# A gated linear recurrence and a SwiGLU block on one core: weights narrowed with one VectorE pass fewer, group 0 begun chunk by chunk, and one more pair of chunks through the 15-product scheme

## The chip, the cores and the metric

The kernel runs on one core of one Trainium2 chip. A core has TensorE (PE, matmuls; the loading of its stationary operand is shown apart as PEld), VectorE (DVE), ScalarE (ACT), GpSimd (POOL) and SyncE (SP), which here only issues DMAs. The metric is the device time of one execution in microseconds (us). The median of three runs of the kernel before is 701.25 us (699.18 to 704.5).

## The reference

```python
def _attn_ref(q, k, v, a_re, a_im):            # (B, H, S, D) = (4, 8, 768, 48)
    mag = np.sqrt(a_re * a_re + a_im * a_im)
    scale = np.minimum(mag, 0.999) / (mag + 1e-06)
    a_re_n, a_im_n = (a_re * scale, a_im * scale)
    for t in range(S):                          # S_re, S_im start at zero
        ar, ai = (a_re_n[:, :, t, :, None], a_im_n[:, :, t, :, None])
        new_re = ar * S_re - ai * S_im
        new_im = ar * S_im + ai * S_re
        kv = np.einsum('bhd,bhe->bhde', k[:, :, t], v[:, :, t])
        S_re, S_im = (new_re + kv, new_im)
        y[:, :, t] = np.einsum('bhd,bhde->bhe', q[:, :, t], S_re)
    return y

def _moe_ref(x, w_gate, w_val, w_out, rms_g):   # x = y as (3072, 384); d_ff = 1536
    rms = np.sqrt(np.mean(x * x, axis=-1, keepdims=True) + 1e-06)
    xn = x / rms * rms_g
    g = xn @ w_gate
    silu = g * (1.0 / (1.0 + np.exp(-g)))
    return silu * (xn @ w_val) @ w_out
```

The activations are float32. The three weight matrices come as float64 and reach the chip as pairs of 32-bit words.

## The kernel before

**Tiling.** The 4 x 768 time steps are cut into 24 chunks of 128 (`C`). Units (`UNITS`) prepare the gates: chunks 0 and 1 are units of one chunk, the others of two. Two chunks form a group (`GROUPS`, 12 of them), which goes through the SwiGLU block together.

**Stages of a chunk.** `gates(u)` turns a_re and a_im into magnitudes and phases (ACT, with several activation tables, and DVE scans), multiplies q and k with them (`rot`), and SP's DMAs reorder the result into the tile `kq`, which the heads read (six DMAs a chunk). `attend(n)` computes masked scores from `kq` (PE, then a COPY_PREDICATED into `am` on DVE), the output y (bank 6, which order and trace number as 71), and the state carried to the next chunk (PE transposes, copies `kt` on ACT, `state` on DVE). The stage "norm" squares y (`sq`), sums it by a matmul with `ones`, makes the mean square `ssv` on DVE and its power -1/2 `rs` on POOL, spreads that over the partitions, by a matmul with `ident` for the first four chunks, and writes the transposed, normalised chunk into `xT`.

**The SwiGLU block.** `feed(g)` is the plain form: for each of six pairs of 128 hidden columns it multiplies `xT` with `wg` and `wv` (12 matmuls with 256 moving columns), ACT takes the silu into `sg`, DVE multiplies into `hT`, and at the end `hT` meets `wo` (24 matmuls of 384 columns for groups 0 and 1). `joint(g)` is the form for the later groups: the 18 block products of a pair of row blocks with the weights' blocks are replaced by 15 products (`PRODUCTS`, in the order of `STEPS`), whose left factors are sums of blocks of `xT` (`X_SUMS`, 12 additions of 128 columns on DVE for each group) and whose right factors are sums of blocks of `wg` and `wv` (`W_SUMS`). `forms()` makes the latter once, 14 sums for each of the two matrices, 512 columns each, partly in place: it can only follow the last plain `feed`. The output product is in seven parts instead of eight (`down`) from group 2 (`FIRST`) on. `PLAIN = 3`: groups 0 to 2 take `feed`, groups 3 to 11 `joint`.

**Weights.** POOL's DMAs fetch them in 12 pieces (six of `wg` and `wv`, 1536 columns of double words each, and six of `wo`, 768 columns) into places in `wo` and `hT` that are free at the start; a piece is issued when the piece before the previous has landed. `narrow(i)` makes float32 of a piece: ACT scales the low words (`Copy`, scale 2^-29), DVE shifts the high words left by 3 (TENSOR_SCALAR), joins the sign and clears two bits (SCALAR_TENSOR_TENSOR), and adds the low word (an integer addition; order shows it as ISA, the trace as CUSTOM_DVE_ANT_0). For groups 0 and 1 the gain `rms_g` (`gcol`) is applied to y; the stage "scale" after group 1 multiplies it into `wg` and `wv`, before the sums. Near the end, `look` reads all weights once more to see that they lie in the range for which this is exact.

**What sets the order.** `Flow` holds every operation with its engine, an assumed duration and a due time, and writes each engine's instructions in the order of a list schedule made while the program is built; on the chip each engine runs its own list in that order and waits by semaphores. Two tables change that order without changing the work: the DMA rate that `dma` assumes, and `flow.shift`, which moves due times by stage and chunk. `send_decays(u)` of units 0 and 1 makes a product `own[u]` on DVE (shown as `ot<-ends,ot`) that a small matmul on PE reads. While PE waits at the start, `flow.warm` puts matmuls on `rot0` without use into its list.

Of the kernel before, what the change touches and what calls it, by code (L numbers as in the profile page):

```python
# [12 lines left out]
BF16 = mybir.dt.bfloat16  # L13
AF = mybir.ActivationFunctionType
# [4 lines left out]
P = 128  # L19
# [698 lines left out]
def fast(tc, ctx, qT, kT, v, a_re, a_im, w_gate, w_val, w_out, rms_g, out, H, bad):  # L718
# [19 lines left out]
    PLAIN = 3  # L738
    WIDE = 12
    SOLO = 6  # L740
# [96 lines left out]
    def dma(o, x, eng="SP", slow=0.0, **kw):  # L837
# [4 lines left out]
        load = n / row * (0.006 + 50.3e-6 * row) / 16  # L842
# [4 lines left out]
        op["packet"] = max(0.07, 0.006 + 50.3e-6 * row * (2 if eng == "POOL" and row == 2048 else 1))  # L847
# [26 lines left out]
    gcol = room("gcol", [P, ND])  # L874
    zeros = room("zeros", [P, 2 * C])
# [71 lines left out]
    dma(gcol, rms_g.rearrange("(c p) -> p c", p=P))  # L947

# [45 lines left out]
    HALVED = ()  # L994

    def narrow(i):
# [8 lines left out]
        act(lo, lo.bitcast(U32), AF.Copy, scale=2.0 ** -29)  # L1005
        step = n // 2 if i in HALVED else n
        for f in range(0, n, step):
            to_, lo_, hi_ = (x[:, :, f:f + step] for x in (t, lo, hi))
            add("DVE", [(nc.vector.tensor_scalar, (),
                         dict(out=to_, in0=hi_, scalar1=3, scalar2=None, op0=ALU.logical_shift_left))],  # L1010
                0.15 + 0.52e-3 * rows * step, [hi_], [to_])
            stt(to_, hi_, 0x3FFFFFFF, to_, ALU.bitwise_or, ALU.bitwise_and)
            tt(to_, to_, lo_, ALU.add)
# [69 lines left out]
    def send_decays(u):  # L1083
        ns = UNITS[u]
        if u < 2:
# [117 lines left out]
    def attend(n):  # L1203
# [75 lines left out]
        if unit_of[n] in LIGHT:  # L1279
            for j in range(ND):  # L1280
                act(yg[:, j], yT[:, j], AF.Copy, scale=gcol[:, j:j + 1])
# [38 lines left out]
    FIRST = 2  # L1320
    WARM = 62.0
# [14 lines left out]
    def feed(g, xT):  # L1336
# [26 lines left out]
        for i in range(2):  # L1363
# [5 lines left out]
            act(ots[i], o, AF.Copy)  # L1369
# [181 lines left out]
    for n in range(N):  # L1551
# [10 lines left out]
        if n == GROUPS[g][-1] and g < WIDE:  # L1562
# [4 lines left out]
            if g == FIRST - 1:  # L1567
# [21 lines left out]
    for in_, limit, op in ((ef, P_MIN, ALU.is_ge), (ef, 1.0, ALU.is_le), (range_, 0.0, ALU.is_le),  # L1589
# [18 lines left out]
        ("attend", 8): 0.6, ("attend", 9): 3.8, ("attend", 11): 3.3, ("attend", 14): 1.6, ("attend", 15): -6.6,  # L1608
        ("attend", 22): 1.5, ("attend", 23): 0.2, ("feed", 4): 13.5, ("feed", 5): 2.3, ("form", 4): 15.0,
        ("form", 12): -0.4, ("look", 3): 1.7, ("look", 6): 70.9, ("look", 7): 45.5, ("look", 8): 38.3,  # L1610
        ("look", 9): 46.0, ("look", 10): 2.2, ("look", 11): -0.3, ("look", 12): 4.4, ("look", 13): 74.9,
        ("look", 14): 75.0, ("look", 15): 69.7, ("look", 16): 45.1, ("look", 17): -3.0, ("norm", 7): 7.5,
        ("norm", 19): -0.1, ("norm", 20): -0.4, ("norm", 21): -1.4, ("norm", 22): -1.4, ("root", 0): -2.0,
        ("root", 3): 21.5, ("root", 8): -10.8, ("rot", 2): -4.7, ("rot", 9): -1.1, ("scale", 0): 2.7,
        ("size", 3): 2.2, ("size", 4): -9.6, ("size", 6): -8.3, ("size", 9): 14.4, ("size", 11): -1.5,
        ("state", 2): -0.3, ("state", 4): -17.0, ("state", 6): -16.7, ("state", 8): -4.3, ("state", 13): -37.5,
        ("state", 14): -11.8, ("state", 15): -8.0, ("state", 19): -14.7, ("state", 22): -0.3, ("turn", 9): 5.8,
# [57 lines left out]
```

## Time and profile before

| | value |
|---|---|
| median of the runs shown | 701.25 us (699.18, 701.25, 704.5) |
| profiled execution, own time | 701.28 us |
| its span, first to last instruction | 699.5 us (1.78 us lie around it) |
| PE busy | 657.1 us, 94% of the span |
| DVE, ACT, POOL busy | 559.4, 477.9 and 59.7 us (80%, 68%, 9%) |
| mean granted TensorE clock | 0.989 |
| chain that ended last, by engine | PE 79%, DVE 7%, ACT 6%, DMA 3%, SP's queue 2%, issue 2% |

All operations are recorded by one line of `Flow` (L715), so rows are told apart by tiles and shapes, not by lines. A matmul of float32 shows as two instructions. Times in the timeline are microseconds from the first instruction; the mean of a group is the time from an instruction's start to its end, and neighbours overlap a little.

### The profile page before, as it was taken

The numbers are of one execution on the slowest core, as the hardware profiler recorded it, in microseconds if no ns is written. First come the engines' busy times: TensorE is split into PE (matmuls) and PEld (weight loads), VectorE is DVE, ScalarE is ACT, GpSimd is POOL, SyncE is SP. The second block draws the span as 40 slices with busy tenths as digits, with TensorE's granted clock in tenths as the row PEclk, the third lists the DMA queues.
The fourth block names the chain that finished last, engine by engine and source line by source line (L and its number), as shares of the span: only waits on it lengthen the run. The fifth ranks groups of instructions, "written<-read, shape, count | busy, mean of one in ns | idle before, by whom it ended". The sixth has DMA issues, their size and how long they took to land.

```text
span 699.5 us, 18714 instructions
## 1 busy us (share of the span) xinstructions
PE 657.1 (94%) x7792; PEld 607.5 (87%) x7792; DVE 559.4 (80%) x1017; ACT 477.9 (68%) x807; POOL 59.7 (9%) x108
## 2 busy tenths in 40 slices
PE   0698999999999999999999999999999998999995
PEld 0587867886889999998999999999999998999995
DVE  8989888869888788888788889888898896356462
ACT  8657777898654675574675684675674884688884
POOL 3122100011000001000101010001000010000000
PEclk9989999999999999999999999999999999999999
DMA  9995462535424243434504334424623543834422
GB/s 292 291 290 178 154 166 75 148 65 106 111 57 103 60 82 62 134 77 86 128 17 80 96 70 96 126 60 86 133 53 75 119 97 112 250 94 145 149 72 91
DMA packets 104012, 81.98 MB, mean 117 GB/s; under 512 B 41936, under 2 KB 94416, under 8 KB 103920
## 3 DMA queue, kind: packets, MB, share of 16 engines
q1 hardware_dynamic: 98560, 64.78, 34.6%
q0 software_dynamic: 4416, 15.35, 10.3%
q8 instruction: 62, 1.02, 0.6%
q10 hardware_dynamic: 944, 0.59, 0.3%
q14 instruction: 30, 0.25, 0.1%
HBM read 55.84 MB, written 4.72 MB: 87 GB/s over the span
## 4 chain that ended last, share of the span: by engine, by line
PE 79%; DVE 7%; ACT 6%; DMA 3%; SPq 2%; issue 2%; POOL 0%; DVEq 0%; ACTq 0%
PE bank L715 79%; SPq L715 2%; DMA kq<-kin 2%; ACT turns L715 2%; ACT L715 1%; DVE hT L715 1%; DVE rot L715 1%; ACT t L715 1%; DVE wv L715 1%; DVE turns L715 1%; DMA in<-in_a_im_dram 1%; DVE wg L715 1%; DMA in<-in_a_re_dram 1%; DVE t L715 1%; DVE in L715 0%
## 5 line engine op out<-in xcount | busy, mean ns | idle before, releaser
L715 PE MATMUL bank<-wo,hT 128*128 128x192 f32 (+1 forms) x696 | 143.7, 352 | 0.9 <-DVE hT L715 0.9
L715 PEld LDWEIGHTS bank<-wo,hT 128*128 128x128 f32 x696 | 115.5, 191 | 13.3 <-DVE hT L715 1.8
L715 PE MATMUL bank<-xT,wg 128*128 128x128 f32 (+1 forms) x504 | 98.2, 330 | 0.0
L715 PE MATMUL bank<-xT,wv 128*128 128x128 f32 (+1 forms) x504 | 94.3, 321 | 0.0
L715 PEld LDWEIGHTS bank<-xT,wg 128*128 128x128 f32 x504 | 80.2, 194 | 7.4 <-issue 0.4
L715 PEld LDWEIGHTS bank<-xT,wv 128*128 128x128 f32 x504 | 79.1, 192 | 5.9 <-ACT turns L715 0.2
L715 ACT ACT_TABLE_LOAD x51 | 65.4, 1283 | 7.3 <-DVE t L715 2.8
L715 ACT ACTIVATE hT<-bank 128x512 f32<-128x512 f32 x90 | 52.4, 594 | 25.9 <-PE bank L715 23.1
L715 POOL TENSOR_TENSOR rs<-ssv,mhalf 128x1 f32<-128x1 f32 x24 | 20.6, 858 | 479.0 <-DVE ssv L715 428.3
L715 ACT ACTIVATE sg<-bank 128x512 f32<-128x512 f32 (+1 forms) x72 | 38.9, 540 | 21.1 <-PE bank L715 17.9
L715 DVE TENSOR_TENSOR hT<-hT 128x768 f32<-128x768 f32 (+1 forms) x58 | 50.5, 871 | 1.1
L715 ACT ACTIVATE bank<-bank 128x512 f32<-128x512 f32 x54 | 31.5, 583 | 26.8 <-PE bank L715 18.9
L715 ACT ACTIVATE kt<-bank 128x384 f32<-128x384 f32 x40 | 19.5, 489 | 43.9 <-PE bank L715 34.8
L715 DVE COPY_PREDICATED am<-causal,bank 128x512 f32<-128x512 int32 x48 | 34.7, 731 | 16.0 <-PE bank L715 15.9
L715 PE MATMUL bank<-yg,wg 128*128 128x128 f32 x288 | 45.7, 281 | 0.0
L715 PE MATMUL bank<-sums,hT 128*128 128x192 f32 x240 | 44.7, 328 | 0.1
L715 PE MATMUL bank<-yg,wv 128*128 128x128 f32 x288 | 43.9, 275 | 0.0
L715 DVE TENSOR_TENSOR hT<-bank,hT 128x512 f32<-128x512 f32 x45 | 30.9, 688 | 14.8 <-ACT bank L715 7.8
L715 PEld LDWEIGHTS bank<-kq 96*32 96x32 f32 x1536 | 31.3, 112 | 12.6 <-issue 4.5
L715 PE MATMUL bank<-kq 96*32 96x128 f32 (+3 forms) x1536 | 37.0, 240 | 5.4 <-DMA kq<-kin 3.6
L715 ACT ACTIVATE turns<-in 128x768 f32<-128x768 f32 (+1 forms) x39 | 30.4, 791 | 13.8 <-DVE kin L715 12.7
L715 PEld LDWEIGHTS bank<-sums,hT 128*128 128x128 f32 x240 | 39.3, 190 | 0.5 <-DVE yg L715 0.2
(216 smaller groups left out, 1417.4 us busy)
## 6 DMA issues: line engine op xcount, KB each, us to landing
kq<-rot SPq DMA_DIRECT2D x90, 128.0 KB, 2.5
kq<-kin SPq DMA_DIRECT2D x54, 128.0 KB, 2.7
kin<-in_q_dram SPq DMA_DIRECT2D x24, 192.0 KB, 3.2
kin<-in_k_dram SPq DMA_DIRECT2D x24, 192.0 KB, 3.4
out_dram<-ot SPq DMA_DIRECT2D x23, 192.0 KB, 2.8
in<-in_a_re_dram SPq DMA_DIRECT2D x11, 384.0 KB, 4.3
in<-in_a_im_dram SPq DMA_DIRECT2D x11, 384.0 KB, 4.2
vn<-in_v_dram SPq DMA_DIRECT2D x20, 192.0 KB, 2.6
```

The source lines that it names most:

```text
L715: fn(*args, **kw)
```

## The change

- `narrow`: the SCALAR_TENSOR_TENSOR is gone. ACT writes the scaled low word as 16 bits and, in a second operation (`Sign`), the sign as a bfloat16 (1 or -1) into the other half of the same word; DVE shifts and adds. This makes the weights half as large; the factor is put back by `gate_col` and `val_col` (from `gcol`) and by the scale of the copies into `ots`.
- `PLAIN = 2`, and with it `LATER = 4`; `SOLO = 4`: group 2 takes `joint`, `forms()` follows group 1, and chunks 4 and 5 use the single buffers of the later chunks.
- `feed` of group 0: the first two of its six blocks (`SPLIT`) multiply each chunk by itself (24 matmuls of 128 columns in place of 12 of 256).
- The DMA rate assumed by the schedule is 41e-6 us a byte and engine instead of 50.3e-6, and `flow.shift` is another table.

```diff
-    PLAIN = 3
+    PLAIN = 2
-    SOLO = 6
+    SOLO = 4
...
-        load = n / row * (0.006 + 50.3e-6 * row) / 16
+        load = n / row * (0.006 + 41e-6 * row) / 16
...
+    MORE = [1.0 if x.dtype == FP32 else 2.0 for x in (w_gate, w_val, w_out)]
+    act(gate_col, gcol, AF.Copy, scale=MORE[0])
+    act(val_col, gcol, AF.Copy, scale=MORE[1] * MORE[2])
...
-        act(lo, lo.bitcast(U32), AF.Copy, scale=2.0 ** -29)
-        step = n // 2 if i in HALVED else n
-        for f in range(0, n, step):
-            to_, lo_, hi_ = (x[:, :, f:f + step] for x in (t, lo, hi))
-            add("DVE", [(nc.vector.tensor_scalar, (),
-                         dict(out=to_, in0=hi_, scalar1=3, scalar2=None, op0=ALU.logical_shift_left))],
-                0.15 + 0.52e-3 * rows * step, [hi_], [to_])
-            stt(to_, hi_, 0x3FFFFFFF, to_, ALU.bitwise_or, ALU.bitwise_and)
-            tt(to_, to_, lo_, ALU.add)
+        low, high = (places[i].bitcast(d).rearrange("p (c f four) -> p c f four", f=n, four=4)[:, :, :, k]
+                     for d, k in ((U16, 0), (BF16, 1)))
+        act(low, lo.bitcast(U32), AF.Copy, scale=2.0 ** -29)
+        act(high, hi.bitcast(FP32), AF.Sign)
+        add("DVE", [(nc.vector.tensor_scalar, (),
+                     dict(out=t, in0=hi, scalar1=3, scalar2=None, op0=ALU.logical_shift_left))],
+            0.15 + 0.52e-3 * rows * n, [hi], [t])
+        tt(t, t, lo, ALU.add)
...
+    SPLIT = 2
...
+                if g == 0 and b < SPLIT:
+                    for t in range(2):
+                        list_ = []
+                        for i in range(2):
+                            f = b * 2 + i
+                            for d in range(ND):
+                                list_.append((o[:, i * T + t * C:i * T + (t + 1) * C],
+                                              w_[:, f // 4, d, f % 4 * P:(f % 4 + 1) * P],
+                                              xT[:, d, t * C:(t + 1) * C], d == 0, d == ND - 1))
+                        dur = 2 * ND * mm_time(C)
+                        clock[0] += dur * SPREAD
+                        mms(list_, dur, due=clock[0] - (1 - t) * dur)
+                    continue
...
-            act(ots[i], o, AF.Copy)
+            act(ots[i], o, AF.Copy, scale=MORE[2])
...
-                    for w_ in (wg, wv):
+                    for w_, col in ((wg, gate_col), (wv, val_col)):
                         for d in range(ND):
-                            act(w_[:, f, d], w_[:, f, d], AF.Copy, scale=gcol[:, d:d + 1])
+                            act(w_[:, f, d], w_[:, f, d], AF.Copy, scale=col[:, d:d + 1])
...
-        ("attend", 8): 0.6, ("attend", 9): 3.8, ("attend", 11): 3.3, ("attend", 14): 1.6, ("attend", 15): -6.6,
+        ("attend", 10): -40.8, ("attend", 13): -20.5, ("attend", 14): 8.5, ("attend", 15): -1.1,
...
```

How the order moves is shown at three places. The first is the start on PE and DVE. PE's list of the kernel before, from its beginning: `bank_66<-ot_134,ot_133` is the matmul of `own[1]`, `rot_105` marks the matmuls without use, and `kq_107` the scores of chunk 0.

```order
L715 MATMUL bank_65<-ot_134,ot_133 96x8 x3
L715 MATMUL bank_68<-rot_105 128x128 x38
L715 MATMUL bank_66<-ot_134,ot_133 96x8 x3
L715 MATMUL bank_68<-rot_105 128x128 x2
L715 MATMUL bank_69<-kq_107 32x128
```

DVE's list before, from the products `rot` of chunk 1 (`rot_106`) to the scores' masks of chunk 0 (`am_115`); `ot_134<-ends,ot_134` is `own[1]`, for which that matmul waits:

```order
L715 TENSOR_TENSOR turns<-turns,t_102 128x2x384 [waits Activation_49]
L715 TENSOR_TENSOR rot_106<-kin,turns 128x768 [waits DMAHW0_49,DVE_49]
L715 TENSOR_TENSOR rot_106<-kin,turns 128x768
L715 ISA wv<-wo,wv 128x3072
L715 TENSOR_SCALAR wg<-wo 128x1536 [waits DMASW1_49]
L715 SCALAR_TENSOR_TENSOR wg<-wo,wg 128x1536 [waits DVE_49]
L715 ISA wg<-wo,wg 128x3072 [waits DVE_49]
L715 TENSOR_TENSOR ends<-t_103,t_102 128x3
L715 TENSOR_TENSOR ot_134<-ends,ot_134 128x24 [waits DVE_49]
```

DVE's list of the change from `own[0]` and `own[1]` (the two rows `ot_136`) to the same masks (`am_117`); `rot_107` and `rot_108` are chunks 0 and 1:

```order
L716 TENSOR_TENSOR ot_136<-ends,ot_136 128x24
L716 SCALAR_TENSOR_TENSOR in_100<-turns 128x384
L716 SCALAR_TENSOR_TENSOR turns<-in_100,zeros 128x128 x3
L716 COPY decay_111<-bank_65 96x8
L716 TENSOR_TENSOR turns<-turns,t_104 128x2x384
L716 TENSOR_TENSOR rot_107<-kin,turns 128x768 x2
L716 SCALAR_TENSOR_TENSOR in_100<-turns 128x384
L716 TENSOR_SCALAR wv<-wo 128x1536
L716 ISA wv<-wo,wv 128x3072
L716 TENSOR_TENSOR turns<-turns,t_104 128x2x384
L716 TENSOR_TENSOR rot_108<-kin,turns 128x768 x2
L716 COPY_PREDICATED am_117<-causal,bank_69 128x512
```

`own[1]` now stands ahead of both chunks' `rot`, no longer behind two pieces' narrowing, and the masks of chunk 0 stand right behind `rot` of chunk 1.

The second place is ACT at the same time, before: `in_98` twice is the two chunks' arctangent, `wo<-wo` the low words of piece 0, and `turns` the phases of chunk 0, which end in two sines.

```order
L715 ACTIVATE in_98<-in_98 128x384 x2
L715 ACTIVATE wo<-wo 128x1536
L715 ACTIVATE turns<-turns 128x384
L715 ACTIVATE in_98<-in_98,mid 128x384
L715 ACTIVATE turns<-in_98 128x384
L715 ACT_TABLE_LOAD
L715 ACTIVATE turns<-in_98 128x384
L715 ACTIVATE turns<-turns,halfpi 128x384
```

And in the change:

```order
L716 ACTIVATE in_100<-in_100 128x384 x2
L716 ACTIVATE wo<-wo 128x1536 x2
L716 ACTIVATE turns<-turns 128x384
L716 ACTIVATE in_100<-in_100,mid 128x384
L716 ACTIVATE gate_col<-gcol 128x3
L716 ACTIVATE turns<-in_100 128x384
L716 ACT_TABLE_LOAD
L716 ACTIVATE turns<-in_100 128x384
L716 ACTIVATE turns<-turns,halfpi 128x384
```

The sign of piece 0 (the second `wo<-wo`) and `gate_col` now stand ahead of chunk 0's sines, and no table load stands between the low words and the sign.

The third place is DVE ahead of the first 15-product group. Before, group 2 is plain, and this is what stands there a little ahead of its first product: the first five weight sums (`in_99`, `rot_106` from `wg`), work of the next unit, and `xT` of chunk 5 (`xT_97`).

```order
L715 SCALAR_TENSOR_TENSOR in_99<-wg 128x512 [waits Activation_49]
L715 TENSOR_TENSOR in_99<-wg,in_99 128x512 [waits DVE_49]
L715 TENSOR_TENSOR rot_106<-wg,in_99 128x512 [waits DVE_49]
L715 SCALAR_TENSOR_TENSOR in_99<-wg,in_99 128x512
L715 TENSOR_TENSOR rot_106<-wg,in_99 128x512 [waits DVE_49]
L715 TENSOR_TENSOR turns<-in_98,turns 128x1536 [waits DMAHW4_49,DMAHW3_49,Activation_49]
```

In the change, the last of a run of 24 weight sums (`wg`, `wv`), then `xT` of chunk 5 (`xT_99`), then the first of the `X_SUMS` (`yg`, `ve`):

```order
L716 TENSOR_TENSOR wg<-wg 128x512
L716 TENSOR_TENSOR wv<-wv 128x512 [waits Activation_49]
L716 TENSOR_TENSOR wg<-wg,in_101 128x512 [waits DVE_49]
L716 TENSOR_TENSOR wv<-wv,kq_110 128x512 [waits DVE_49]
L716 TENSOR_SCALAR t_103<-t_103 128x768 [waits Activation_49]
L716 TENSOR_TENSOR turns<-in_100,turns 128x1536 [waits DMAHW7_49,DMAHW0_49]
L716 TENSOR_TENSOR xT_99<-bank_71,row 128x3x128 [waits DMASW7_49]
L716 TENSOR_TENSOR yg_127<-xT_99 128x128
L716 TENSOR_TENSOR yg_128<-xT_99 128x128 [waits DVE_49]
```

So 24 of the 28 weight sums, where five stood before, and the `X_SUMS` of a group come ahead of group 2.

More of the change, by code (lines that the diff above doesn't have):

```diff
@@ L13 @@
 BF16 = mybir.dt.bfloat16
+U16 = mybir.dt.uint16
 AF = mybir.ActivationFunctionType
@@ L846, in dma @@
         op["load"] = load
-        op["packet"] = max(0.07, 0.006 + 50.3e-6 * row * (2 if eng == "POOL" and row == 2048 else 1))
+        op["packet"] = max(0.07, 0.006 + 41e-6 * row * (2 if eng == "POOL" and row == 2048 else 1))
         return op
@@ L874, in fast @@
     gcol = room("gcol", [P, ND])
+    gate_col = room("gate_col", [P, ND])
+    val_col = room("val_col", [P, ND])
     zeros = room("zeros", [P, 2 * C])
@@ L992, in fetch @@
         return words[:, :, 0], words[:, :, 1]
-    HALVED = ()
     def narrow(i):
@@ L1084, in send_decays @@
         ns = UNITS[u]
+        flow.stage = "decay", u
         if u < 2:
@@ L1280, in attend @@
             for j in range(ND):
-                act(yg[:, j], yT[:, j], AF.Copy, scale=gcol[:, j:j + 1])
+                act(yg[:, j], yT[:, j], AF.Copy, scale=gate_col[:, j:j + 1])
         else:
```

16 lines of the change are left out of this document (7 added, 9 removed), and 3 rows, old and new, of the table filler.

## The prediction

> **What bounds the kernel now.** I read the page's busy times and its chain that ended last, then a table by stage, then the list of PE's waits, and the timeline where they stand. The page first:
>
> ```profile
> PE 657.1 (94%) x7792; PEld 607.5 (87%) x7792; DVE 559.4 (80%) x1017; ACT 477.9 (68%) x807; POOL 59.7 (9%) x108
> PE 79%; DVE 7%; ACT 6%; DMA 3%; SPq 2%; issue 2%; POOL 0%; DVEq 0%; ACTq 0%
> ```
>
> PE is the bound of the whole, and 42.4 us of the span (699.5 less 657.1) are without it. The stages (length, then PE, PEld, DVE, ACT, POOL busy, the granted clock, DMA share, GB/s) say where:
>
> ```profile
> 0.00:35.47 35.47, 11.22 (x82) 10.93 (x82) 31.55 (x60) 25.59 (x41) 9.26 (x32) 1.00 0.95 293
> 35.47:55.88 20.41, 17.18 (x334) 15.24 (x334) 18.39 (x21) 10.91 (x19) 6.65 (x7) 0.83 1.09 299
> 55.88:176.70 120.82, 119.24 (x1174) 94.34 (x1174) 101.44 (x151) 97.61 (x133) 12.19 (x19) 0.99 0.47 119
> 176.70:232.70 56.00, 56.00 (x602) 49.77 (x600) 48.66 (x78) 29.38 (x41) 3.38 (x6) 1.00 0.38 89
> ...
> 232.70:692.80 460.10, 453.46 (x5609) 437.19 (x5602) 358.79 (x709) 314.37 (x576) 28.23 (x44) 1.00 0.40 99
> ```
>
> Up to 55.88, where group 0 begins, most PE work is idle matmuls and the chunks 0 and 1; DVE and the DMAs are full. From 55.88 on PE is busy but for 1.6 us up to group 2 (176.70), 0 in it, and 6.6 us behind. So a gain comes from an earlier 55.88, from fewer PE microseconds behind it, or from those few stalls. The list of PE's waits (total, times, longest):
>
> ```profile
> PE bank L715 <- DVE ot L715: 20.0, 2, 17.0
> ...
> PE bank L715 <- DMA kq<-kin: 3.8, 3, 2.5
> PE bank L715 <- POOL rs L715: 2.9, 2, 2.3
> PE bank L715 <- DMA kq<-rot: 1.1, 1, 1.1
> ...
> PE bank L715 <- DMA vn<-in_v_dram: 0.4, 1, 0.4
> ```
>
> **The start.** PE's timeline (start, length, operation, in brackets the idle time ahead of it):
>
> ```profile
> 35.47 1.13 PE L715 MATMUL bank<-ot,ot 128*96 128x8 f32 x6 [3.06 <-DVE ot L715]
> ...
> 37.59 2.36 PE L715 MATMUL bank<-kq 96*32 96x128 f32 x64
> ...
> 44.83 1.33 PE L715 MATMUL bank<-kq 96*32 96x128 f32 x64
> 46.77 0.49 PE L715 MATMUL bank<-ident,rs 128*128 128x128 f32 x2 [0.61 <-POOL rs L715]
> ...
> 54.75 0.49 PE L715 MATMUL bank<-ident,rs 128*128 128x128 f32 x2 [2.25 <-POOL rs L715]
> ```
>
> The scores of chunk 0 (37.59) stand behind the matmul of `own[1]`, which waits for DVE until 35.47. What chunk 0 itself needs is here (timelines of ACT, DVE, SP and POOL, then the DMA view of 0 to 60 us):
>
> ```profile
> 14.81 1.57 ACT L715 ACTIVATE wo<-wo 128x1536 int32<-128x1536 uint32 x1
> 16.28 0.52 ACT L715 ACTIVATE turns<-turns 128x384 int32<-128x384 f32 x1
> ```
>
> ```profile
> 21.31 1.83 DVE L715 TENSOR_TENSOR rot<-kin,turns 128x768 f32<-128x768 f32 x2
> ...
> 27.17 1.83 DVE L715 TENSOR_TENSOR rot<-kin,turns 128x768 f32<-128x768 f32 x2
> ```
>
> ```profile
> 22.30 3.86 SPq L715 DMA_DIRECT2D kq<-rot  x6
> ...
> 29.37 3.81 SPq L715 DMA_DIRECT2D kq<-rot  x6
> ```
>
> ```profile
> 33.31 0.17 POOL L715 COPY seen<-kq 96x1 f32<-96x1 f32 x1
> ```
>
> ```profile
> kq<-rot SPq DMA_DIRECT2D x12, 128.0 KB, 5.7
> ```
>
> Chunk 0's six `kq` transfers are issued until 26.2, the last one's issue begins near 25.6, and with 5.7 us to land they are there at about 31.3, by 33.3 at the latest, where POOL reads them. The change takes `own[1]` out of the way but puts piece 0's sign on ACT ahead of chunk 0's phases. A second 1536-column pass there costs 1.47 us (16.28 less 14.81), so `rot` of chunk 0 begins near 22.9, `kq` is issued from 23.9 to 27.8 and lands at 32 to 34. I take 33: 4.6 us ahead of 37.59.
>
> Chunk 1 follows chunk 0. DVE has in both lists one shift and one 1.75 us operation of a piece between the two `rot` (the addition now, the joining pass before), so `rot` of chunk 1 also moves by about 1.5 us, SP issues from 31 to 34.8, and `kq` lands near 40, up to 42.5 with a slow transfer. PE now has chunk 0's `ident,rs` ahead of chunk 1's scores; that stood 9.2 us behind chunk 0's scores (46.77 less 37.59), so it comes near 42.2, and chunk 1's scores near 42.4 instead of 44.83. From there to group 0 were 11.05 us (55.88 less 44.83), with 2.25 us of waiting for `rs`, which stays. Begun chunk by chunk, group 0 need not wait for chunk 1's `xT` and the idle matmuls behind 54.75, some 0.7 us. DVE and ACT have reordered pieces around it, so I give back 0.2: group 0 begins near 52.9, **3.0 us earlier**. The bounds are 0 (the sign and late `kq` take everything) and 5.3 (4.6 plus 0.7). Weights are not late there: block 0 and 1 need the first two pieces only.
>
> **Products.** In the timeline, plain products and 15-product blocks at full pace, and the group of weight loads:
>
> ```profile
> 62.83 2.75 PE L715 MATMUL bank<-xT,wg 128*128 128x256 f32 x12
> 65.42 2.75 PE L715 MATMUL bank<-xT,wv 128*128 128x256 f32 x12
> ...
> 247.00 0.61 PE L715 MATMUL bank<-xT,wg 128*128 128x128 f32 x4
> 247.45 0.61 PE L715 MATMUL bank<-xT,wv 128*128 128x128 f32 x4
> ```
>
> ```profile
> L715 PEld LDWEIGHTS bank<-xT,wg 128*128 128x128 f32 x504 | 80.2, 194 | 7.4 <-issue 0.4 <-ACT hT L715 0.2 <-DVE xT L715 0.2
> ```
>
> Twelve instructions take 2.59 us (0.2158 each), four small ones 0.447 (0.1118). Group 2 now has 144 of the first (72 matmuls), 31.1 us; with 15 products it has 240 of the second, 26.8 us: **4.24 us less**. Against that, the split blocks of group 0 turn 48 instructions of 0.2158 into 96 of 0.1118, 0.37 more, and one more seeding of a bank stands in PE's list, 0.2 (row below: 176.48 to the group's 176.70). Net 3.65 less. PE is busy for 98.6% of the stage in which the nine groups now run so (453.46 of 460.10), so it counts in full.
>
> The Trainium skill ("TensorE: Matmul & The Clock Gate", section "Back-to-back issue gap") speaks against it: sustained, 128 columns cost about 81 ns and 512 about 131, so a small product is dear for its size because its weight load is paid as well. By a line between these, an estimate, 256 columns would be some 98 ns, so 240 small products would take 19.4 us against 14.1 for 144 large ones, and in that proportion group 2 would grow by some 11.7 us instead of losing 4.24. The rows above have half the time for half the columns: for these float32 products the trace does not agree.
>
> **Stalls that go.** Two of PE's waits between 55.88 and 176.70:
>
> ```profile
> 93.58 1.33 PE L715 MATMUL bank<-kq 96*32 96x128 f32 x64 [1.10 <-DMA kq<-rot]
> ...
> 101.41 0.88 PE L715 MATMUL bank<-vn,kt 128*32 128x48 f32 x48 [0.38 <-DMA vn<-in_v_dram]
> ```
>
> `kq` and `vn` of chunk 2 are late by 1.1 and 0.4 us. With the joining passes gone DVE reaches chunk 2's `rot` several microseconds sooner, and SP's list has `vn` of chunk 2 between chunk 1's `kq`. I take **1.5 us less** (bounds 0 and 1.5; if PE is 3 us earlier and DVE isn't, the stall grows by up to 3 instead, which is in the range's upper part). The 6.4 us of stalls behind 232.70, of which `kq<-kin` is the largest part, I leave alone: the work there is the same, in a changed order. Chunks 4 and 5 now use the single buffers too; the later chunks that do so have 3.8 us of waits for `kq<-kin` between them, some 0.2 a chunk. I keep plus or minus 3 for all of it.
>
> **DVE and ACT.** These groups price the narrowing, the sums of the weights and of the activations, and an activation table's load:
>
> ```profile
> L715 DVE SCALAR_TENSOR_TENSOR wv<-wo,wv 128x1536 int32<-128x1536 int32 x2 | 3.5, 1758 | 0.1
> ...
> L715 DVE SCALAR_TENSOR_TENSOR wo<-hT,wo 128x768 int32<-128x768 int32 x4 | 3.8, 952 | 0.0
> ...
> L715 DVE TENSOR_TENSOR wg<-wg 128x512 f32<-128x512 f32 x4 | 2.7, 687 | 0.1
> ...
> L715 DVE TENSOR_TENSOR yg<-xT 128x128 f32<-128x128 f32 x45 | 11.3, 283 | 0.0
> ```
>
> ```profile
> L715 ACT ACT_TABLE_LOAD x51 | 65.4, 1283 | 7.3 <-DVE t L715 2.8 <-issue 2.2 <-DVE kin L715 1.4
> ```
>
> Twelve joining passes go from DVE: six of 1.758 and six of about 0.952 us, 16.3 us, of which some 7.5 lie behind 55.88. ACT gets twelve signs, by the low words' 1.57 some 15 us, 7 behind 55.88. Ahead of group 2 stand 19 more weight sums (13.1 us at 0.687) and 12 `X_SUMS` (3.4). So from group 0 to group 2 DVE has 101.4 - 7.5 + 13.1 + 3.4 = 110.4 us, and ACT 97.6 + 7 = 104.6, of some 119 us in which PE works. Both fit, with 9 us of DVE to spare instead of 19; the two small operations for `gate_col` and `val_col` and the scale of copies that are there anyway are hidden by ACT's 14.
>
> What matters is the end of that stretch. The sums can only follow group 1's last products, since they overwrite `wg` and `wv`:
>
> ```profile
> 154.57 2.75 PE L715 MATMUL bank<-xT,wv 128*128 128x256 f32 x12
> ...
> 176.48 0.39 PE L715 MATMUL bank<-zeros 128*128 128x512 bf16 x1
> ```
>
> From the end of these (157.3) to the seeding ahead of group 2 PE has 19 us of attention and output product. DVE has to do there about 21 sums (14.6 us), two operations of the next unit (2.7) and the first `X_SUMS`: 17.3 us and a little. It just fits, if DVE doesn't arrive late; before, the same run of sums stood ahead of group 3 and cost PE no stall. I take **0.8 us** of new wait, between 0 and 17.3 (all cover gone), near 0 because of that.
>
> The Trainium skill ("ScalarE: Activation LUTs", section "Rules for kernel authors") has it that simple element-wise operations belong on VectorE. Here the rows give 1.57 us on ACT for what was 1.76 on DVE, in float32, so the move itself is not dearer. In its section "Table sets: the hidden batching unit" that page of the Trainium skill names copies among what is in each set, and the sign not. If the sign needed a set of its own, a load there and back on chunk 0's path would take 2.6 us of the gain (twice 1.283); the built program has no load beside the signs.
>
> **The sum.** 699.5 - 3.0 - 3.65 - 1.5 + 0.8 = 692.15 for the span; 1.78 us lie around it (701.28 own time): **693.9 us**. The profiled execution stands at the median shown (701.25), so nothing is shifted. 1% is about what a measurement of this kernel can tell from no change; here that is 694.2 and 708.3.
>
> **Rivals.**
> 1. *More gain.* `kq` lands as soon as 31.3 does now, so the start gains its 5.3 (2.3 more), and up to 4 of the later 6.4 us of stalls go with DVE's lighter load: 687.5 to 690.5. For it: DVE loses 16.3 us. Against it: most of that lies at the start, and DMAs, at a share of 0.95 to 1.09 there, don't get faster.
> 2. *The start gains nothing.* The sign holds up ACT, `kq` of chunk 1 lands at its slow end, and `rs` on POOL stays behind it: 693.9 + 3.0 = 696.9, up to 699 if the waits of chunk 2 stay too. For it: DMA is full up to 55.88.
> 3. *The other side: the weight sums are not covered.* `wg` and `wv` are multiplied by the gain on ACT, then summed on DVE, and group 2 needs the sums. If DVE comes to 157.3 with its 9 spare microseconds used up, each further one is a stall; without any cover 17.3 us, 693.9 - 0.8 + 17.3 = 710.4. From 8.2 us of stall on the kernel is slower than before. For it: DVE is 93% full ahead of that point. Against it: the run that stalled nothing before group 3.
> 4. *Small products pay their weight loads.* A load lasts 0.194 us; 240 of them one after another are 46.6 us, 15.5 more than the plain group: about 713. Against it: nine groups run at 0.112 already. The rule of the Trainium skill told above ("TensorE: Matmul & The Clock Gate") sides with this one.
> 5. *The change does little of what it says*: new stalls of the reordered list eat products and start alike, 699 to 702.
>
> **How the numbers follow.** The forecast (690.5 to 696.9) has 0.50, six in ten of it below 694.2; the rivals 0.20, 0.18, 0.07, 0.02 and 0.03. Faster by over 1%: 0.30 + 0.20 = 0.50. Slower by over 1%: 0.03 of the third and the fourth's 0.02, 0.05. Within: 0.45. The range takes in the first, second and fifth and leaves out most of the third, the fourth and a little below the first: 687 to 700.5.
>
> **What would show it.** Group 0's first product at 52 to 54 us, the scores of chunk 0 near 33 with `kq<-rot` as what they wait for, not `ot`; group 2 as 120 small matmuls at 0.112 an instruction, and ahead of it a wait of PE for DVE (`yg` or `wg`) under 2 us; no wait at chunk 2's scores; no table load beside a sign. Wrong would be the forecast if group 0 begins at 55 or later, or if the waits behind group 3 come to more than 9 us or fewer than 3.

## The result, and the profile after

The change makes the kernel **slower: 722.8 us** (median of four runs, 722.16 to 724.84) against 702.7 us for the kernel before on the same chip. The ratio is 1.0297, with a 95% interval of 1.0248 to 1.0347. The forecast was 693.9 us. The page of the profiled execution (span 721.5 us) begins so, busy times first and then the chain that ended last:

```profile
PE 659.3 (91%) x7905; PEld 609.5 (84%) x7905; DVE 556.9 (77%) x1037; ACT 529.0 (73%) x842; POOL 57.8 (8%) x108
PE 71%; ACT 19%; DVE 4%; DMA 3%; issue 2%; SPq 1%; POOL 0%; DVEq 0%; ACTq 0%
```

PE has about as much to do as before, but is idle for 62.2 us instead of 42.4. ACT is busy for 51.1 us more, where 15 were expected, and its share of the chain went from 6% to 19%. The table by stage has the same three cuts as before: up to group 0, up to group 2, and the rest of the products.

```profile
0.00:66.32 66.32, 27.86 (x385) 25.35 (x385) 41.85 (x74) 63.24 (x66) 13.96 (x39) 0.84 0.84 252
66.32:203.14 136.82, 125.29 (x1215) 98.45 (x1215) 103.43 (x159) 112.82 (x135) 11.58 (x20) 0.94 0.41 103
203.14:714.80 511.66, 506.11 (x6312) 485.71 (x6307) 411.41 (x805) 352.94 (x643) 32.26 (x50) 1.00 0.40 99
```

Group 0 begins at 66.32 instead of 55.88, and ACT is busy for 63.24 us of that stretch, 95%. From group 0 to group 2 it takes 136.82 us instead of 120.82. From group 2 to the end of the span it takes 518.4 us (721.5 less 203.14) instead of 522.8: there the change gains its 4.4. PE's list of waits now has ACT high in it, where before it had 0.3 us for ACT's `kt`:

```profile
PE bank L716 <- ACT kt L716: 8.0, 2, 5.1
PE bank L716 <- ACT sg L716: 6.0, 1, 6.0
```

What ACT does is seen in its timeline at the start, and in the groups of the narrowing passes:

```profile
14.95 7.23 ACT L716 ACTIVATE wo<-wo 128x1536 uint16<-128x1536 uint32 x2
21.93 0.57 ACT L716 ACTIVATE turns<-turns 128x384 int32<-128x384 f32 x1
...
34.49 10.80 ACT L716 ACTIVATE hT<-hT 128x1536 uint16<-128x1536 uint32 x3
45.01 0.60 ACT L716 ACTIVATE kt<-bank 128x384 f32<-128x384 f32 x1
```

```profile
L716 ACT ACTIVATE wo<-wo 128x1536 bf16<-128x1536 f32 x4 | 14.6, 3650 | 0.1
L716 ACT ACTIVATE wo<-wo 128x1536 uint16<-128x1536 uint32 x4 | 14.5, 3624 | 0.0
L716 ACT ACTIVATE hT<-hT 128x768 bf16<-128x768 f32 x4 | 7.8, 1961 | 0.0
```

The sign of 1536 columns lasts 3.65 us, not 1.57. The low word, whose result is now 16 bits wide, lasts 3.62 us, where it lasted 1.62 before. Piece 0's two passes take 7.23 us ahead of chunk 0's phases (21.93; 16.28 before). Later three passes in a row keep chunk 0's `kt` waiting until 45.01, and PE with it. The price does not end there, as PE's timeline shows at two later places (the first waits for ACT; the second, the start of group 1, waits for the norm of chunk 3, and e1 below has a shorter wait there too):

```profile
95.03 5.31 PE L716 MATMUL bank<-xT,wg 128*128 128x256 f32 x12 [6.03 <-ACT sg L716]
...
142.03 0.79 PE L716 MATMUL bank<-ident,rs 128*128 128x128 f32 x2 [2.32 <-POOL rs L716]
143.47 4.99 PE L716 MATMUL bank<-xT,wg 128*128 128x256 f32 x12 [0.65 <-DVE xT L716]
```

Twelve instructions of 256 columns take 2.75 us at full pace; behind these two waits they take 5.31 and 4.99, some 2.4 us more, and the granted clock of the middle stage is 0.94. The Trainium skill ("TensorE: Matmul & The Clock Gate", section "What's actually happening") has PE begin at half the clock and reach the full one after a few microseconds of steady work; the trace agrees here, with a granted clock of 0.50 from 95.03 to 97.70 us and of 1.00 from 100.30 on. But not every wait costs the clock. The same place in e9 and in e10, two kernels of the experiments below:

```profile
76.79 5.49 PE L717 MATMUL bank<-xT,wg 128*128 128x256 f32 x12 [3.07 <-ACT sg L717]
...
77.20 2.86 PE L717 MATMUL bank<-xT,wg 128*128 128x256 f32 x12 [3.08 <-ACT sg L717]
```

So the length of a wait alone does not tell what follows it.

### The profile page after: what moved, and what is told of

Read it like the earlier page. It is cut to its first block, busy times and chain, and to the rows that moved or that the text cites. A ratio compares the mean times of both kernels' runs of the same rounds, so it can differ in the third digit from the quotient of the medians.

```text
span 721.5 us, 19000 instructions
## 1 busy us (share of the span) xinstructions
PE 659.3 (91%) x7905; PEld 609.5 (84%) x7905; DVE 556.9 (77%) x1037; ACT 529.0 (73%) x842; POOL 57.8 (8%) x108
## 4 chain that ended last, share of the span: by engine, by line
PE 71%; ACT 19%; DVE 4%; DMA 3%; issue 2%; SPq 1%; POOL 0%; DVEq 0%; ACTq 0%
PE bank L716 71%; ACT wo L716 4%; ACT hT L716 4%; ACT L716 2%; ACT t L716 2%; ACT turns L716 2%; DMA kq<-kin 1%; ACT in L716 1%; DVE hT L716 1%; DMA rot<-in_w_val_dram 1%; DVE turns L716 1%; ACT rot L716 1%; SPq L716 1%; ACT bank L716 1%; DMA in<-in_a_re_dram 1%
## 5 line engine op out<-in xcount | busy, mean ns | idle before, releaser
L716 PE MATMUL bank<-xT,wg 128*128 128x128 f32 (+1 forms) x488 | 90.4, 321 | 6.7 <-ACT sg L716 6.0
L716 PEld LDWEIGHTS bank<-xT,wg 128*128 128x128 f32 x488 | 74.9, 202 | 12.8 <-ACT sg L716 6.6
L716 PE MATMUL bank<-xT,wv 128*128 128x128 f32 (+1 forms) x488 | 82.5, 301 | 0.0
L716 ACT ACTIVATE hT<-bank 128x512 f32<-128x512 f32 x100 | 58.4, 593 | 29.2 <-PE bank L716 26.2
L716 PEld LDWEIGHTS bank<-xT,wv 128*128 128x128 f32 x488 | 70.2, 192 | 3.2
L716 PE MATMUL bank<-yg,wg 128*128 128x128 f32 x320 | 51.3, 283 | 0.0
L716 PE MATMUL bank<-yg,wv 128*128 128x128 f32 x320 | 48.8, 275 | 0.0
L716 ACT ACTIVATE sg<-bank 128x256 f32<-128x256 f32 (+1 forms) x72 | 38.6, 536 | 9.3 <-PE bank L716 7.0
L716 PEld LDWEIGHTS bank<-yg,wg 128*128 128x128 f32 x320 | 42.2, 191 | 2.2 <-issue 0.8
L716 PEld LDWEIGHTS bank<-yg,wv 128*128 128x128 f32 x320 | 42.2, 192 | 0.0
```

Source lines behind the costliest of these rows:

```text
L716: fn(*args, **kw)
```

## The experiments

The theory after the first look was that ACT's passes with 2-byte results cost everything. Its rivals were the number of passes and the new order. This table holds where each profiled execution has group 0's and group 2's first product (from PE's timelines, us) and the measured medians and ratios, which later paragraphs use:

| kernel | group 0 begins | to group 2 | from there | span | median | ratio to before (95%) |
|---|---|---|---|---|---|---|
| before | 55.9 | 120.8 | 522.8 | 699.5 | 702.7 | |
| the change | 66.3 | 136.8 | 518.4 | 721.5 | 722.8 | 1.0297 (1.0248 to 1.0347) |
| e1 wide writes | 52.1 | 130.1 | 520.9 | 703.1 | 703.3 | 1.0003 (0.9973 to 1.0033) |
| e2 old narrowing, new list | 57.6 | 132.9 | 530.5 | 721.0 | 720.0 | 1.0237 (1.0220 to 1.0254) |
| e3 new narrowing alone | 66.8 | 133.0 | 523.8 | 723.6 | 727.3 | 1.0356 (1.0337 to 1.0374) |
| e5 no sign | 51.9 | 126.9 | 518.9 | 697.6 | 701.0 | 0.9979 (0.9956 to 1.0001) |
| e6 old narrowing, same order | 58.4 | 125.6 | 518.8 | 702.8 | 705.4 | 1.0030 (0.9998 to 1.0063) |
| e7 half | 57.1 | 132.8 | 521.5 | 711.5 | 710.5 | 1.0108 (1.0075 to 1.0142) |
| e8 told | 63.5 | 144.0 | 532.8 | 740.2 | 739.9 | 1.0506 (1.0441 to 1.0570) |
| e9 narrow, 4 bytes apart | 51.4 | 130.4 | 523.0 | 704.8 | 704.9 | 1.0030 (0.9999 to 1.0060) |
| e10 e9, norm 3 early | 52.5 | 129.7 | 524.0 | 706.2 | 700.6 | 0.9977 (0.9953 to 1.0001) |
| e11 e6, norm 3 early | 58.4 | 123.5 | 522.1 | 703.9 | 702.8 | 1.0010 (0.9982 to 1.0039) |
| e12 e1, light pieces | 52.2 | 123.1 | 522.3 | 697.5 | 698.2 | 0.9917 (0.9879 to 0.9956) |
| e13 e12, norm 3 early | 51.5 | 121.8 | 518.7 | 691.9 | 695.9 | 0.9924 (0.9895 to 0.9953) |
| e14 e10, piece 11 behind kq | 52.4 | 122.7 | 521.0 | 696.1 | 696.7 | 0.9933 (0.9901 to 0.9964) |
| e15 e11, piece 11 behind kq | 58.7 | 119.4 | 518.0 | 696.1 | 698.7 | 0.9958 (0.9929 to 0.9986) |

A profiled execution is one of several and need not take the median time (e10's span is 706.2 us beside a median of 700.6, e13's 691.9 beside 695.9), so the columns of the spans tell of places, not of totals. Medians of the kernel before moved between 701.2 and 702.8 us from one set of runs to the next; the ratios allow for that.

### Is it the width of the writes?

e1 writes whole words, in the instruction order of the change:

```diff
-        act(low, lo.bitcast(U32), AF.Copy, scale=2.0 ** -29)
-        act(high, hi.bitcast(FP32), AF.Sign)
+        act(lo, lo.bitcast(U32), AF.Copy, scale=2.0 ** -29)
+        act(lo.bitcast(FP32), hi.bitcast(FP32), AF.Sign)
```

> The changed kernel, but ACT writes its two results (the scaled low word, then the sign) as whole 4-byte words, the second over the first; the last three bits of every weight are left out by that. Same number of ACT and DVE passes, same waits. Theory W (an ACT pass that writes 2-byte elements 8 bytes apart lasts 3.65 us for 1536 columns where a 4-byte write lasts 1.62, and that alone costs the time): the passes fall to about 1.6 and 0.9 us, ACT busy falls from 529 to about 493 us, group 0 begins near 53 us, and the time is near the forecast, 692 to 698 us. Theory S (twelve more ACT passes ahead of chunk 0 and in group 0 are too many, at any width): the time stays above 708. Theory R (the rest of the change, its order above all, loses the time): 715 or more.

703.3 us: 19.5 below the change with the same passes in the same order. So the loss lies in how these passes write, and theories S and R fall (e4 and e9 below tell the width from the distance). ACT is busy for 494.8 us, and group 0 begins at 52.05, near the forecast's 52.9. A piece's low words and signs, 1536 columns each, take 3.34 us together, where piece 0's took 7.23:

```profile
54.91 3.34 ACT L716 ACTIVATE wo<-wo 128x1536 int32<-128x1536 uint32 x2 [1.61 <-DMA wo<-in_w_gate_dram]
```

But the expected 692 to 698 us is missed by 5 us, which is the second question below.

e2 and e3 exchange the narrowing and let the schedule list everything anew:

```diff
 # e2, the change with before's narrowing; e3 does the reverse in the kernel before
-        act(high, hi.bitcast(FP32), AF.Sign)
+            stt(to_, hi_, 0x3FFFFFFF, to_, ALU.bitwise_or, ALU.bitwise_and)
```

> The changed kernel with the narrowing of before (three VectorE passes, one ACT pass with 4-byte writes); all the rest of the change stays. Theory W: the time is below the kernel before, 692 to 699 us, since the products' 4.2 us and part of the start are gained. Theory R: 705 or more, because the loss stays when the narrowing goes back. If DVE's three passes hold up the weight sums, PE shows a wait for DVE of several us ahead of group 2.

> The kernel before with the narrowing of the change alone (and the factor put back). Theory W: ACT busy grows from 478 to about 530 us and the time to 715 to 730 us, with PE waiting for ACT (kt, sg) ahead of group 2. Theory R: within 1% of the kernel before, 695 to 709.

e3 has the loss in full, 727.3 us. e2 did not lose it: 720.0 us, although its passes are those of before. By itself that speaks for theory R. The table shows where e2 is slow: it is 8 us behind even after group 2, where narrowing is long over. So e6 put the same old narrowing into the order of the change:

```diff
+        add("ACT", [], 0.17 + 0.86e-3 * rows * n, [hi], [lo])      # the sign's place, empty
         add("DVE", [(nc.vector.tensor_scalar, ...),
+                    (nc.vector.scalar_tensor_tensor, ...)], 0.15 + 0.52e-3 * rows * n, [hi], [t])
```

> The narrowing of before (three VectorE passes, one ACT pass with 4-byte writes) put into the instruction order of the changed kernel: the joining pass stands right behind the shift on VectorE, the sign's place on ACT is empty, everything else stands where the change has it. In e2 the same work was listed anew by the schedule and took 720 us. Theory O (e2 was slow because of its order, not because of the work): 696 to 704 us. Theory D (DVE's 16.3 us of joining passes are what the order of the change can't bear): 712 to 722 us, with PE waiting for DVE ahead of group 0 and of chunk 2.

705.4 us, just above theory O's range (696 to 704) and far below theory D's: 14.6 us less than e2 for the same work. A list made anew, with the same table of shifts, can lose that much without any cause in the edit. e8 shows it from the other side:

```diff
-        dur = 0.17 + 0.86e-3 * cols(o) + ...
+        dur = (0.27 + 2.2e-3 * cols(o) if 2-byte result else 0.17 + 0.86e-3 * cols(o)) + ...
```

> The changed kernel, its schedule told what a 2-byte write costs on ACT (0.27 us and 2.2 ns a column, from the groups of e4, where it assumed 0.17 and 0.86); the work is the same, the order is made anew with it. Theory P (the loss is in the work on ACT, whatever the order): 716 to 726 us. Theory O (the order, made with too small a duration, is a large part of it): 706 to 714 us.

Neither theory: the schedule that knows the true duration makes a kernel 17 us slower still, 739.9 us. The shifts of due times belong to one list, so from here on all kernels keep the list of the change.

e4 measured the disputed passes by themselves (names: w32 and f32 are 4-byte results 8 bytes apart, h16 and b16 are 2-byte ones 8 apart, q16 2-byte 4 apart, c16 and d16 2-byte without gaps):

```diff
+            act(out=every(b16, 4)[:, :n], in_=hi.bitcast(FP32)[:, :n], func=AF.Sign)   # and so on, three of each
```

> A kernel of its own that leaves out the whole computation and writes zeros: ACT passes of 1536 and 768 columns in groups of three, with 4-byte or 2-byte results, 2, 4 or 8 bytes apart, then copies on DVE. Theory W1 (the 2-byte element written with gaps is what is slow): w32s8 and f32s8 about 1.5 to 1.6 us, h16s8 and b16s8 about 3.65, c16s2 and d16s2 (no gaps) about 1.5. Theory W2 (the conversion to 16 bits is slow): c16s2 and d16s2 are about 3.6 as well. Theory W3 (reading and writing the same words in place is slow): h16s8 and b16s8, which lie in a tile of their own here, are about 1.6.

```profile
L64 ACT ACTIVATE b16s<-raw 128x1536 bf16<-128x1536 f32 x3 | 10.7, 3578 | 0.0
L56 ACT ACTIVATE h16s<-raw 128x1536 uint16<-128x1536 uint32 x3 | 10.7, 3577 | 0.0
...
L58 ACT ACTIVATE q16s<-raw 128x1536 uint16<-128x1536 uint32 x3 | 5.8, 1917 | 0.0
...
L54 ACT ACTIVATE w32s<-raw 128x1536 int32<-128x1536 uint32 x3 | 4.8, 1603 | 0.0
L66 ACT ACTIVATE d16s<-raw 128x1536 bf16<-128x1536 f32 x3 | 4.8, 1593 | 0.0
L62 ACT ACTIVATE f32s<-raw 128x1536 f32<-128x1536 f32 x3 | 4.7, 1576 | 0.0
L60 ACT ACTIVATE c16s<-raw 128x1536 uint16<-128x1536 uint32 x3 | 4.6, 1533 | 0.0
```

W1: neither the 16 bits (1.53 and 1.59 us without gaps) nor the gap (1.60 and 1.58 with 4-byte results) nor work in place is slow, but the 2-byte result with a gap: 3.58 us at 8 bytes apart and 1.92 at 4.

Two kernels with the full computation confirm it as a dose. e7 narrows the sign alone, e9 puts both results 4 bytes apart:

```diff
 # e7
-        act(low, lo.bitcast(U32), AF.Copy, scale=2.0 ** -29)
+        act(lo, lo.bitcast(U32), AF.Copy, scale=2.0 ** -29)
 # e9: results go into the weight's own place, the high word is shifted where it lies
-        act(low, lo.bitcast(U32), AF.Copy, scale=2.0 ** -29)
-        act(high, hi.bitcast(FP32), AF.Sign)
+        act(out=t16[:, :, :, 0], in_=lo.bitcast(U32), func=AF.Copy, scale=2.0 ** -29)
+        act(out=tb[:, :, :, 1], in_=hi.bitcast(FP32), func=AF.Sign)
```

> The changed kernel with the low word written as 4 bytes and the sign, as in the change, as 2 bytes: the same result and the same order, but one narrow write a piece instead of two. The change lies at 722.8 us and e1, with none, at 703.3. If the loss is proportional to ACT's extra time: ACT busy about 511 us and 711 to 715 us. If there is a threshold (cover that is used up first): within 3 us of either.

> The changed kernel with its two narrow writes 4 bytes apart instead of 8: ACT writes the low word and the sign straight into the weight's own place, VectorE shifts the high word where it lies and adds. Same result, same number of passes, the same order but for one ACT pass of piece 7, which stands a little later because its place must be free. e4 had 1.92 and 1.06 us for such passes (3.58 and 1.88 at 8 apart, 1.60 and 0.92 for 4-byte writes). Theory W (the loss is the duration of these passes): ACT busy about 500 us and 702 to 707 us, near e1's 703.3. If something else in the narrow writes costs the time (the words next to the ones being read, say): 712 or more.

e7: ACT busy 511.7 us, time 710.5 us, just under the 711 to 715 of a proportional loss and far from both ends; half of ACT's extra time costs 7.2 of the 19.5 us, so the price is a dose but not strictly proportional. e9: ACT busy 498.9 us and 704.9 us. The narrowing in two DVE passes with 2-byte results is there in full, and costs what e1 costs, within the intervals.

### Where did the forecast's gain go in e1?

In e1 group 0 begins 3.8 us sooner than before, and the stretch to group 2 is 9.3 us longer. PE's timeline has two places in it:

```profile
90.20 2.36 PE L716 MATMUL bank<-kq 96*32 96x128 f32 x64 [4.57 <-DMA kq<-rot]
...
121.82 0.49 PE L716 MATMUL bank<-ident,rs 128*128 128x128 f32 x2 [1.10 <-POOL rs L716]
122.95 4.54 PE L716 MATMUL bank<-xT,wg 128*128 128x256 f32 x12 [0.65 <-DVE xT L716]
```

Chunk 2's `kq` is late by 4.57 us (1.10 before), and group 1 waits twice for the norm of chunk 3. Both are followed by slow matmuls. Is the first ACT's doing, through the signs, or the DMAs'? e5 leaves out the sign passes, e12 most of two weight transfers:

```diff
 # e5
-        act(lo.bitcast(FP32), hi.bitcast(FP32), AF.Sign)
-        ... scalar1=3, scalar2=None, op0=ALU.logical_shift_left
+        ... scalar1=3, scalar2=0x3FFFFFFF, op0=ALU.logical_shift_left, op1=ALU.bitwise_and
 # e12, for pieces 10 and 11
+            sent["calls"] = [(nc.gpsimd.dma_start, (), dict(out=raw3[:, :, 0:f8], in_=src[:, :, 0:f8]))]
```

> The kernel of e1 (4-byte writes) with the twelve sign passes left out, all other instructions in the same order on each engine; the weights lose their sign by that (VectorE's shift masks it off in the same pass). e1 lost its gain at chunk 2, where PE waits 4.6 us for kq, and ahead of group 1. Theory L (ACT, busy 95% from 52 to 90 us, brings chunk 2's phases late because of the signs): chunk 2's kq comes 3 to 5 us sooner, the wait falls under 1.5 us, and the time is 692 to 698 us. Theory Q (the kq transfers land late because the DMAs are busy with weights, 6.6 us in the median in e1 against 4.9 before): the wait stays above 3.5 us and the time within 2 us of e1's 703.3.

> The kernel of e1 (4-byte writes), with the transfers of the last two weight pieces, 10 and 11, cut to an eighth of their columns: the rest of these weights is left over from other pieces and wrong. Everything else, the order too, is as in e1, where PE waits 4.57 us for kq of chunk 2 while piece 11 is under way and kq lands 6.6 us after its issue. Theory Q (these weights and kq share the DMAs, and that makes kq late): kq lands in under 4.5 us, the wait falls under 2 us, the time to 698 to 701. Theory L (kq is issued late, from rot, and lands as it does in any case): the wait stays above 3.5 us and the time at 702 to 705.

e5 did not decide: 701.0 us and the wait left over lie between the two theories. The scores of chunk 2 come 2.45 us sooner, and PE still waits 3.02 us. e12 did: 698.2 us. These are the scores of chunk 2 in e5 and in e12, and what the `kq` tile's view of e12 says of the transfers from 74 to 95 us, chunk 2's six and chunk 3's six behind them:

```profile
87.75 1.47 PE L716 MATMUL bank<-kq 96*32 96x128 f32 x64 [3.02 <-DMA kq<-rot]
...
87.62 1.33 PE L716 MATMUL bank<-kq 96*32 96x128 f32 x64 [1.51 <-DMA kq<-rot]
```

```profile
DMA to landing us min/median/max: 2.3/3.1/4.7
```

In e1 that view (78 to 92 us) has 2.3/6.6/7.6. Piece 11's transfer is issued in e1 at 81.39 and lands by 89.4, over the same time as the six transfers of chunk 2. PE's wait of 4.57 us falls to 3.02 without the signs and to 1.51 with the light pieces: the signs on ACT have a part in it, the shared DMAs the larger one.

For the second place e10 and e11 move the norm of chunk 3 by hand, in the finished list:

```diff
     flow.schedule()
+    early = [o for o in flow.ops if o["stage"] == ("norm", 3) and o["eng"] != "ACT"]
+    for o, at in zip(early, (448.5, 448.6, 448.7, 456.5, 457.5)):
+        o["order"] = at
```

> e9, and the stage norm of chunk 3 is moved by hand in the finished order: its sum of squares on PE stands 8 output products earlier, its mean square, root, spreading matmul and xT follow earlier as well; nothing else moves. In e1, e5, e6 and e7 alike PE waits 1.10 us for rs and 0.65 us for xT ahead of group 1 and then runs its first 12 products in 4.5 us instead of 2.75. Theory N (this stretch of the order costs 3 to 4 us): both waits go, the first 12 products take about 2.8 us, and the time falls by 3 to 4 us against e9. Rival: what waits next takes its place (chunk 4's kq, which the moved operations delay by 0.7 us on VectorE), and it falls by less than 1.5.

> The kernel of e6 (the narrowing of before in the order of the change, 705.4 us) with norm of chunk 3 moved in the same way. Theory N: 701 to 703 us, level with the kernel before. Rival as in e10: 704 or more.

700.6 us against e9's 704.9, and 702.8 against e6's 705.4. In e10 the start of group 1 is this, with no wait and at full pace:

```profile
121.98 0.38 PE L717 MATMUL bank<-ident,rs 128*128 128x128 f32 x2
...
123.75 0.39 PE L717 MATMUL bank<-zeros 128*128 128x512 bf16 x1
123.98 2.75 PE L717 MATMUL bank<-xT,wg 128*128 128x256 f32 x12
```

e10 fell by 4.3 us, a little more than theory N's 3 to 4. e11 lies in its own range of 701 to 703, 2.65 us below e6, whose first products had run in 2.86 us already, so that only the waits could go. The intervals of e6 and e11 overlap, so for the old narrowing this gain is likely, not shown.

Left open was whether the two places are all of it. e13 takes both away from e1; e14 and e15 have the full computation and send piece 11 only when `kq` of chunk 2 has landed:

```diff
+    sent11["calls"] = [(nc.gpsimd.tensor_copy, (), dict(out=seen, in_=kqs[0][0:D2, 0, 0:1]))] + sent11["calls"]
+    sent11["order"] = 332.5
```

> The kernel of e12 (4-byte writes, the transfers of the last two pieces cut to an eighth, so their weights are wrong) with norm of chunk 3 moved as in e10. If the two places are all that kept e1 (703.3) from the forecast (693.9): 703.3 - 5.1 - 4.3 = 693.9, so 692.5 to 695.5. If they overlap (a wait taken away at chunk 2 comes back at group 1 or later): 697 or more.

> e10 (narrow writes 4 bytes apart, norm of chunk 3 early; the full computation), and the last weight piece's transfer is issued only when kq of chunk 2 has landed: POOL first reads one column of kq. Its two ACT passes and VectorE's shift stand later in their lists to match. Theory Q: kq lands 1.5 to 3 us sooner, PE's wait at chunk 2 falls by as much, 697.5 to 699.5 us (e10: 700.6). Rival: piece 10 and the other loads fill the DMAs as well, or the late piece holds up ACT or the output product: 700 or more.

> e11 (the narrowing of before, norm of chunk 3 early, 702.8 us) with the last piece behind kq of chunk 2 as in e14. Theory Q: 700 to 701.5. It stays above e14, because group 0 begins at 58.4 us in it (PE waits 7.5 us for rs, VectorE's joining passes ahead of it), not at 52.5.

e13 took 695.9 us, just above its range, and its ratio is that of e12 within the intervals: e12, with `kq` nearly in time, still had both waits for the norm (1.09 and 0.65 us), but its group 1 began at the full clock (2.86 us for the first twelve), so the norm was worth less. So the two places overlap in part. The forecast's ratio, 693.9 to 701.28 or 0.9895, is the lower end of e13's interval; some 2 us may be missing still, and no run here says where. **e14 beats both kernels: 696.7 us**, 0.9933 of the kernel before (0.9901 to 0.9964), a gain of 0.7%. PE's wait at chunk 2 is 0.90 us in it, and the twelve `kq` transfers land in 2.5 us in the median (at most 7.5, a transfer of chunk 3 that now meets piece 11):

```profile
88.48 1.33 PE L717 MATMUL bank<-kq 96*32 96x128 f32 x64 [0.90 <-DMA kq<-rot]
```

e15, with the old narrowing, has 698.7 us, under its range of 700 to 701.5. It stays 2 us above e14, as far as the intervals tell anything, and as expected it begins group 0 six microseconds later (58.7 us).

## Why the prediction was wrong, step by step

- **The step that failed is a term of "DVE and ACT"**: "ACT gets twelve signs, by the low words' 1.57 some 15 us". The row it was taken from is a pass with 4-byte results 8 bytes apart. The signs have 2-byte results 8 bytes apart: 3.65 us for 1536 columns and 1.96 for 768, 33.6 us in all. The low words, which the prediction left at their price, got the same kind of result and went from 15.4 to 33.5 us. So ACT got 51.7 us and not 15. That was in the diff (`BF16`, `U16`, every fourth element), and no row of the trace of before had such a write. It was a cost to bound from both sides, and it was taken from the nearest row as if that were its own. e1 against the change puts its price at 19.5 of the 28.9 us between the forecast and the measured time; most of the rest lies at chunk 2 and at group 1, below.
- **The weighing against the Trainium skill** ("ScalarE: Activation LUTs", section "Rules for kernel authors") compared 1.57 us on ACT with 1.76 on DVE. With 3.65 us the trace stands on the side of the Trainium skill, for a reason that the rule doesn't give. On table loads the prediction was right: 45 loads, none beside a sign.
- **The start, 3.0 us**: the steps hold where the writes are wide. Group 0 begins at 52.05 us in e1 and at 51.4 in e9, where 52.9 was forecast. With the old narrowing in the same order (e6) it begins at 58.4, later than before, so in this order the early start needs the lighter DVE. In the change itself piece 0's two passes bring chunk 0's phases 5.7 us later (21.93 less 16.28) instead of 1.47, and the next pieces hold up `kt`.
- **Products, net 3.65 us**: right in the rates. Twenty-four instructions of 128 columns take 2.67 us (from 70.44 to 73.11 in the change), 0.11 each, so the rival of small products that pay for their weight loads did not come. The total is less sure: from group 2 on the change takes 4.4 us less than before, e5 and e6 3.9 and 4.0, but e1 1.9, and e9 0.2 more. Waits for later `kq` and the clock move that stretch as well; PE's busy time in it is 509.5 us before, 506.1 in the change and 508.0 in e9.
- **Stalls that go, 1.5 us**: wrong. `vn` was in time, but chunk 2's `kq` waited longer than before in e1 (4.57 us). The step looked at when `rot` is ready, not at what shares the DMAs with `kq` behind it (e12).
- **The weight sums, 0.8 us**: within the bounds, but too dear. In the change no wait stands ahead of group 2's first product at 203.14, nor in e1 ahead of 182.18. (21 sums at 0.687 us are 14.4 us, not 14.6.)
- **Missing in the sum**: the start of group 1, some 3.5 us in e1, e5, e7 and e9 (1.10 and 0.65 of waiting, 1.8 of slow products), and the waits alone, 1.75 us, in e6 and e12. It could have been read from the list, where only some 2 us of PE's work stand between chunk 3's sum of squares and its `ident,rs`. Only the start and group 2 were looked up there. And each wait's price was taken as its idle time alone.
- Of the rivals, none was this one. "The start gains nothing" named ACT and the sign, at a price of 3.0 us; 13.4 would have been needed (66.3 less 52.9).

## What to carry to other kernels

Price an operation by the form of its result too: element size and distance, not columns alone. If no row of the trace has that form, the nearest row is a bound and not a price, and one short kernel of bare passes settles it before anything is built on it. When a stage is moved forward, ask what its transfers will meet on the DMAs, and what stands ahead of the next consumer in the list. And where a schedule is made anew by every edit, compare edits in one fixed order: here the order alone moved the time by 15 us.

## What the runs showed of the hardware

- ACT, 1536 columns: 2-byte results 8 bytes apart 3.58 us, 4 apart 1.92, without gaps 1.53 to 1.59; 4-byte results 8 apart 1.58 to 1.60. From the two sizes (3.58 and 1.88 us) a column costs 2.2 ns in the first case and 0.88 (1.60 and 0.92) with 4-byte results.
- The Trainium skill ("SBUF — State Buffer", section "Door 1: The DMA port swizzle (why `[64,N]` ≈ `[32,N]`)") has lines of 16 bytes and asks for two hits on each for full pace; 2-byte elements 8 bytes apart, two to a line, should then be free. For ACT's writes the measurement differs: 2-byte results are slow at that distance, and 4-byte ones at the same distance are not.
- DVE lost by the same gap, though less. Its copies to bfloat16 in e4, 8 bytes apart and without gaps, and a 4-byte copy 8 apart:

```profile
L73 DVE CAST v16s<-g32s 128x1536 bf16<-128x1536 f32 x3 | 5.6, 1867 | 87.3 <-ACT g32s L70 87.3
...
L75 DVE CAST u16s<-g32s 128x1536 bf16<-128x1536 f32 x3 | 3.0, 996 | 0.0
L77 DVE COPY v32s<-g32s 128x1536 f32<-128x1536 f32 x3 | 3.0, 994 | 0.0
```

- SP's twelve `kq` transfers of chunks 2 and 3, 128 KB each, land in 2.5 to 4.3 us in the median where the weight piece of 768 KB beside them is sent later or cut (e14 2.5, e13 3.0, e12 3.1, e15 4.3), and in 5.7 to 7.0 where it is under way with them (e10 5.7, e5 6.1, e1 6.6, e9 6.8, e6 7.0).
- Waits of the same length are followed by different clocks: behind 3.07 us of waiting e9's next twelve instructions of 256 columns take 5.49 us, behind 3.08 us e10's take 2.86. No run here says what decides it.
